# Regrouping the attention's products on TensorE: scores, values of two groups back, then transposes

## The chip, the cores and the metric

The kernel runs on one core of a Trainium2 chip. Its time is the device time of one execution in microseconds; of the kernel before there are three runs: 883.45, 883.65 and 884.38 us, median 883.65. Five engines work at once and meet by semaphores: TensorE (PE, products), VectorE (DVE), ScalarE (ACT), GpSimd (POOL) and SyncE (SP), whose queue issues most of the transfers.

## The reference

Windowed attention over 4 sequences of 576 positions with 8 heads of 64, then two dense networks on the 2304 positions:

```
scores = q @ k^T / 8, allowed where 0 <= query - key < 64
attn   = exp(scores - max) / (sum + 1e-9)
x      = attn @ v, heads side by side: 2304 x 512
x      = ((x @ w1) * (x @ w2)) @ w3 @ w_out          # w1, w2: 512 x 1024; w3: 1024 x 1024
h      = x @ w_in                                    # 512 x 2048
out    = (h * sigmoid(h)) @ w_out2                   # 2048 x 512
```

The weights are float64 arrays; their words are converted to float32 on the chip.

## The kernel before, in words

Attention is cut into 72 groups: 18 stretches of 128 positions times 4 pairs of heads, numbered so that the groups 12b to 12b+11 make up the 384 positions of block b (NBLK = 6 blocks). A group goes through these functions: `scores` (product of q and k into PSUM tile `s`, then on DVE, line 275, mask and row minimum into `sm`), `exps` (ACT, line 286), `normalise` (DVE: add, reciprocal and the multiply of line 298), `transposes` (three products with the identity, PSUM tile `t`, line 308), `split_t` (ACT and DVE bring the transposed weights to SBUF), `values` (product with v into PSUM tile `o`, and its sum into `xr`). Groups 0 to 16 are "plain" (float32 products, lines 261 and 335 to 337, a copy of `o` by ACT, line 338); the other 55 split each operand into a high and a low part (fp32r; lines 265, 269, 343, 344) and sum four parts of `o`: two ACT copies (347, 348), two DVE additions (349, 350), a POOL addition (351). `prep_qk` and `prep_v` make the high and low parts of q, k (ACT 240, POOL 244, DVE 247) and v (helper `split`, lines 79 and 82).

The program is in hand-written order: each engine executes its instructions in the order in which the code issues them. `half(2g)` and `half(2g+1)` issue the two halves of group g, and `halves_to` puts a half between other products. Three phases do so:

- `phase_w` (to about 104 us): DVE, ACT and POOL convert weight words (lines 114, 115, 125, 128, 132; the high and low parts at 140, 144), PE forms w3 x w_out (line 476, `accw`), and the first 28 halves run between. `fill` puts conversion steps between the steps of a softmax.
- `phase_a(b)`, one per block: 16 units of 12 products with w1, w2 (line 504, `ab`), then 8 units of 12 products with the formed weights (line 524, `x`). Before each of the 24 units one half of attention for the next block is issued, so a block carries twelve groups. Its input is `xr` split by `split_x` into `xa`, `xb`, a quarter at a time, in units 17, 19, 21 and 22 of the block before.
- after the last block, the second network (lines 627, 646).

PSUM holds one `s`, one `t` and one `o` tile; once the conversions of the first phase are done, odd groups use the tile `z` as a second `o`.

Of the kernel before, what the change touches and what calls it, by code (L numbers as in the profile page):

```python
# [42 lines left out]
def tile_window_attention_ffn(ctx, tc, qkv, vp, mask, ident, w1, w2, w3t, w_out, w_in, w_out2, out):  # L43
# [142 lines left out]


    NG = NU * NPAIR
    LAST_HALF = 2 * NG + 2
    qk_raw, v_raw, qk_st, v_st, s_st, p_st = {}, {}, {}, {}, {}, {}  # L190
    pt = {}

# [132 lines left out]
    def values(g):  # L325
        u, c = place(g)
        r = u % 3 * 128

        tag = "z" if done["step"] == len(line) and g % 2 else "o"
        o_ps = psa.tile([128, 2, 2, 128], F32, name=f"o{g}", tag=tag)  # L330
        if plain(g):


            v, p, o = v_p[g % 3], p_st.pop(g), o_ps[:, 0, 0]
            nc.tensor.matmul(o, lhsT=v[:, 0:128], rhs=p[:, 0:128], start=True, stop=False)
            nc.tensor.matmul(o, lhsT=v[:, 64:192], rhs=p[:, 128:256], start=False, stop=False)
            nc.tensor.matmul(o[:, 0:64], lhsT=v[:, 192:320], rhs=p[:, 256:320], start=False, stop=True)
            nc.scalar.copy(out=xr[:, c, r : r + 128], in_=o)
            return
        vhl = v_st.pop(g)  # L340
        b, a = pt[g % 2, 1], pt[g % 2, 0]
        for h in range(2):
            nc.tensor.matmul(o_ps[:, h], lhsT=vhl[:, h], rhs=b[:, h], start=(h == 0), stop=False)  # L343
        nc.tensor.matmul(o_ps[:, :, :, 0:64], lhsT=vhl[:, 2], rhs=a, start=False, stop=True)  # L344
        o_ps = o_ps.rearrange("p h t n -> p h (t n)")
        t = att.tile([128, 256], F32, name=f"ot{g}", tag="ot", bufs=1)
        nc.scalar.copy(out=t[0:64], in_=o_ps[64:128, 0, :])
        nc.scalar.copy(out=t[64:128], in_=o_ps[0:64, 1, :])
        nc.vector.tensor_tensor(out=t[0:64], in0=o_ps[0:64, 0, :], in1=t[0:64], op=ALU.add)
        nc.vector.tensor_tensor(out=t[64:128], in0=o_ps[64:128, 1, :], in1=t[64:128], op=ALU.add)  # L350
        nc.gpsimd.tensor_tensor(out=xr[:, c, r : r + 128], in0=t[:, 0:128], in1=t[:, 128:256], op=ALU.add)  # L351

    def half(h):


        g, odd = divmod(h, 2)
        if not odd:
            t_ps = transposes(g - 1) if 1 <= g <= NG else None
            if g < NG:
                scores(g)  # L360
            if t_ps is not None:
                split_t(g - 1, t_ps)
            if g < NG:
                exps(g)
        else:
            if g < NG:
                normalise(g)
            if 1 <= g <= NG:
                values(g - 1)
            for x in (g + 1, g + 2):  # L370
                if x - g == (1 if plain(x - 2) else 2):
                    prep_qk(x)
            if g < NG:
                prep_v(g)

            for x in range(g + 2, g + 5):
                if g < (x - 2 if plain(x - 2) else x - 4):
                    break
                load_qk(x)
            for x in range(g + 1, g + 4):  # L380
                if g < (x - 2 if plain(x - 3) else x - 3):
                    break
                load_v(x)

    halves = [0]

    def halves_to(n):
        while halves[0] < min(n, LAST_HALF):
# [3 lines left out]
    def split_x(blk, c):  # L392
        if c == 0:
            xhl[blk] = [slot(f"{t}{blk}", t, [2, 2, NB], F32R) for t in ("xa", "xb")]
        x = xhl[blk][c // 2][:, c % 2]
        split(x[:, 0], x[:, 1], xr[:, c], "dve", "dve" if blk else "pool")


    W_HALVES = 28
# [1 line left out]
    def phase_w():  # L401
# [58 lines left out]
        for s in range(16):  # L460
            sw, j = divmod(s, 8)
            loads_to(ready[s + 2] + (3 if s > 1 else 0))
            if j == 0:
                for i in range(4):
                    acc[i] = accumulator(f"accw{sw}_{i}", [128, 512])
            for part in range(2):
                first = ready[s + 1 if s else 0]
                steps_to(first + (ready[s + 2] - first) * (part + 1) // 2, (nc.vector, nc.gpsimd), 3)
                halves_to(min(W_HALVES, 2 + W_HALVES * (2 * s + part + 1) // 32))
                for c in range(4):  # L470
                    if halves[0] >= 6 * c + 8 and (0, c) not in split_done:
                        split_done.add((0, c))
                        split_x(0, c)
                fill(3)
                for i in (0, 1) if part == 0 else (2, 3):
                    nc.tensor.matmul(  # L476
                        acc[i], lhsT=w3x[s % 7][:, i * 128 : (i + 1) * 128], rhs=wo[:, j],
                        start=(j == 0), stop=(j == 7),
                    )
                    if j == 7:  # L480
                        n = sw * 4 + i
                        wp[n] = slot(f"wp{n}", f"w{16 + n}", [2, 512], F32R)
                        split(wp[n][:, 0], wp[n][:, 1], acc[i], "act", "dve")
# [272 lines left out]
```

## Time and profile before

| | |
|---|---|
| median of the runs | 883.65 us (883.45 to 884.38, 3 runs) |
| profiled execution | 884.13 us |
| its span, first to last instruction | 882.3 us |
| PE busy | 856.0 us, 97% |
| DVE, ACT, POOL busy | 480.7, 491.0, 430.6 us |
| mean granted TensorE clock | 0.997 of full speed |

The span is the time between the first and the last instruction of the profiled execution. A product's record begins when PE starts it and overlaps the next one's, so starts, not lengths, give its price. Stretches are in microseconds from the span's start. In a row of waits stands who waited, for whom, the total, how often, and the longest.

### The profile page before, as it was taken

Reading aid. Unit: us, or ns where it says so; the run is one execution under the profiler, and the core shown is the slowest. Engines: PE = TensorE matmul, PEld = TensorE weight load, DVE = VectorE, ACT = ScalarE, POOL = GpSimd, SP = SyncE. Lnnn points to the kernel's source line nnn. Section 1 sums busy time; section 2 is a strip of 40 time slices with the busy share of each in tenths; the row PEclk is TensorE's granted clock in tenths of the full one; section 3 lists DMA queues with packets and bytes.
Section 4 is the critical chain, followed back from the end, with each engine's and each line's share of the span. In section 5 each row is a group of like instructions: output and inputs, shape, how many; then the busy total and the mean of one; then the engine's idle time right before and its main releaser. Section 6 shows DMA issues by size and latency. Waiting matters only on the chain.

```text
span 882.3 us, 13255 instructions
## 1 busy us (share of the span) xinstructions
PE 856.0 (97%) x4362; PEld 737.0 (84%) x4362; DVE 480.7 (54%) x1202; ACT 491.0 (56%) x1219; POOL 430.6 (49%) x474
## 2 busy tenths in 40 slices
PE   4998999999999999999999999999999999999997
PEld 2454689999999999999999888888888888888896
DVE  5889888878888888888365886111111111111111
ACT  5778677788787788787475775222222222222322
POOL 4558476466466466465395787222322232222222
PEclk9999999999999999999999999999999999999999
DMA  8888423333432323331477500200020001000100
GB/s 286 295 251 262 134 79 99 125 99 100 127 94 90 126 90 100 119 99 50 182 277 261 202 0 1 77 20 0 1 89 7 0 1 51 22 0 1 48 1 25
DMA packets 43205, 85.84 MB, mean 97 GB/s; under 512 B 4864, under 2 KB 22528, under 8 KB 43136
## 3 DMA queue, kind: packets, MB, share of 16 engines
q1 hardware_dynamic: 37088, 75.55, 26.4%
q10 hardware_dynamic: 6048, 9.44, 2.9%
q8 instruction: 35, 0.57, 0.3%
q14 instruction: 34, 0.28, 0.1%
HBM read 75.53 MB, written 9.44 MB: 96 GB/s over the span
## 4 chain that ended last, share of the span: by engine, by line
PE 86%; DVE 2%; POOL 1%; issue 1%; ACT 0%; DMA 0%; POOLq 0%; SPq 0%; DVEq 0%
PE h L627 23%; PE o L646 22%; PE ab L504 21%; PE x L524 11%; PE t L308 2%; PE o L343 2%; PE s L265 1%; PE s L269 1%; PE accw L476 1%; PE o L344 1%; POOL klo L244 1%; DVE cv_b L128 0%; DVE cv_z L125 0%; DVE rs L294 0%; PE s L261 0%
## 5 line engine op out<-in xcount | busy, mean ns | idle before, releaser
L82 POOL TENSOR_TENSOR g<-sg,g 128x512 fp32r<-128x512 f32 (+1 forms) x80 | 94.8, 1185 | 250.0 <-ACT g L79 237.3
L627 PE MATMUL h<-x2t,hl 128*128 128x512 f32 (+1 forms) x960 | 213.4, 371 | 0.0
L646 PE MATMUL o<-hl,g 128*128 128x512 f32 x864 | 211.2, 392 | 0.4 <-ACT g L79 0.3
L633 DVE TENSOR_TENSOR sg<-h,sg 128x512 f32<-128x512 f32 (+1 forms) x80 | 51.1, 638 | 288.5 <-ACT sg L632 288.5
L627 PEld LDWEIGHTS h<-x2t,hl 128*128 128x128 f32 x960 | 169.4, 188 | 33.8
L646 PEld LDWEIGHTS o<-hl,g 128*128 128x128 f32 x864 | 160.9, 188 | 35.9 <-ACT g L79 0.8
L632 ACT ACTIVATE sg<-h 128x512 f32<-128x512 f32 (+1 forms) x80 | 44.4, 555 | 195.4 <-PE h L627 195.4
L504 PE MATMUL ab<-xa,hl 128*128 128x384 f32 x576 | 117.1, 338 | 0.0
L504 PE MATMUL ab<-xb,hl 128*128 128x384 f32 x576 | 115.6, 335 | 0.0
L504 PEld LDWEIGHTS ab<-xb,hl 128*128 128x128 f32 x576 | 101.4, 188 | 0.0
L504 PEld LDWEIGHTS ab<-xa,hl 128*128 128x128 f32 x576 | 99.8, 188 | 0.8
L351 POOL TENSOR_TENSOR xr<-ot 128x128 f32<-128x128 f32 x55 | 33.2, 603 | 118.5 <-DVE ot L350 116.5
L132 POOL TENSOR_TENSOR cv_b<-cv_b,cv_r 128x512 int32<-128x512 int32 x48 | 73.6, 1534 | 26.8 <-DVE cv_b L128 11.2
L79 ACT CAST g<-sg 128x512 fp32r<-128x512 f32 (+1 forms) x80 | 46.3, 579 | 63.5 <-DVE sg L633 61.8
L286 ACT ACTIVATE sm<-sm,nm 128x192 f32<-128x192 f32 x144 | 64.4, 448 | 17.7 <-DVE nm L275 16.6
L244 POOL TENSOR_TENSOR klo<-qk,qkhi 64x192 fp32r<-64x192 f32 x110 | 70.1, 637 | 5.7 <-ACT qkhi L240 1.5
L524 PE MATMUL x<-p,wp 128*128 128x384 f32 x360 | 69.6, 335 | 0.0
L524 PEld LDWEIGHTS x<-p,wp 128*128 128x128 f32 x360 | 62.2, 188 | 0.1
L125 DVE TENSOR_SCALAR cv_z<-cv_b 128x512 int32<-128x512 int32 x72 | 49.4, 686 | 17.0 <-ACT cv_b L114 16.6
L114 ACT ACTIVATE cv_b<-words 128x512 f32<-128x512 f32 x72 | 48.2, 670 | 11.5 <-DMA words<-in_w_out 5.6
L128 DVE SCALAR_TENSOR_TENSOR cv_b<-words,cv_z 128x512 int32<-128x512 int32 x72 | 49.4, 686 | 3.5 <-issue 0.5
L275 DVE CUSTOM_DVE_ANT_0 sm<-s,mask_sb 128x192 f32<-128x192 f32 x144 | 45.7, 354 | 6.6 <-PE s L261 3.6
(82 smaller groups left out, 1258.9 us busy)
## 6 DMA issues: line engine op xcount, KB each, us to landing
qk<-in_qkv SPq DMA_DIRECT2D x55, 384.0 KB, 3.1
words<-in_w_out SPq DMA_DIRECT2D x24, 512.0 KB, 8.4
words<-in_w3t SPq DMA_DIRECT2D x16, 512.0 KB, 6.2
words<-in_w SPq DMA_DIRECT2D x16, 512.0 KB, 6.2
words<-in_w_in SPq DMA_DIRECT2D x16, 512.0 KB, 6.8
v<-in_qkv SPq DMA_DIRECT2D x55, 96.0 KB, 2.7
x2d<-x2s ACTq DMA_DIRECT2D x24, 192.0 KB, 1.9
out_x<-osb ACTq DMA_DIRECT2D x18, 256.0 KB, 2.1
```

Source lines behind the costliest of these rows:

```text
L82: (nc.vector if eng_lo == "dve" else nc.gpsimd).tensor_tensor(out=lo, in0=src, in1=f32(hi), op=ALU.subtract)
L114: nc.scalar.activation(out=f32(self.b), in_=f32(self.high), func=AF.Copy, scale=2.0**-112)
L125: nc.vector.tensor_scalar(out=self.z, in0=b, scalar1=3, scalar2=None, op0=ALU.logical_shift_left)
L128: nc.vector.scalar_tensor_tensor(out=b, in0=self.high, scalar=-0x80000000, in1=self.z, op0=ALU.bitwise_and, op1=ALU.bitwise_or)
L132: nc.gpsimd.tensor_tensor(out=x, in0=b, in1=self.r, op=ALU.add)
L244: nc.gpsimd.tensor_tensor(out=k_lo[g % 2][hs, h * 192 : h * 192 + 192], in0=t[hs, n], in1=f32(hi[hs, n]), op=ALU.subtract)
L286: nc.scalar.activation(out=x, in_=x, func=AF.Exp, scale=-1.0, bias=nm[:, h : h + 1], accum_out=rs[:, h : h + 1])
L504: nc.tensor.matmul(acc, lhsT=w[:, l, fs], rhs=x[k // 2][:, k % 2, r, :], start=(k == 0 and n == 0), stop=(k == 3 and n == 2),)
L524: nc.tensor.matmul(acc, lhsT=wp[f][:, l, o * 128 : (o + 1) * 128], rhs=p[f][:, r, :], start=(f == 0 and n == 0), stop=(f == 7 and n == 2),)
L627: nc.tensor.matmul(acc, lhsT=weights["in", f // 4, k][:, l, fs], rhs=x[:, k, r, :], start=(k == 0 and i == 0), stop=(k == 3 and i == 2),)
L633: nc.vector.tensor_tensor(out=sg, in0=acc, in1=sg, op=ALU.mult)
L646: nc.tensor.matmul(oacc[t], lhsT=g[:, l, t * 128 : (t + 1) * 128], rhs=weights["out", f][:, r, :], start=(f == 0 and i == 0), stop=(f == 1 ...
```

## The change

On PE, the two clusters of a group (transposes of g-1 and scores of g in the even half, values of g-1 in the odd half) become one in the even half: scores of g, values of g-2, transposes of g-1. The sum of `o` is no longer issued by `values` itself: it is returned as a function and issued in the odd half behind `normalise`; at a block's last group it is issued at the end of the even half. There is one half more in all (`LAST_HALF`). The load of v is issued one group later for plain groups. `split_x` takes ACT for the high part and POOL for the low part in all blocks, and in the first phase it waits for two more halves.

```diff
--- before.py
+++ after.py
@@ -186,7 +186,7 @@
 
 
     NG = NU * NPAIR
-    LAST_HALF = 2 * NG + 2
+    LAST_HALF = 2 * NG + 3
     qk_raw, v_raw, qk_st, v_st, s_st, p_st = {}, {}, {}, {}, {}, {}
     pt = {}
 
@@ -335,38 +335,45 @@
             nc.tensor.matmul(o, lhsT=v[:, 0:128], rhs=p[:, 0:128], start=True, stop=False)
             nc.tensor.matmul(o, lhsT=v[:, 64:192], rhs=p[:, 128:256], start=False, stop=False)
             nc.tensor.matmul(o[:, 0:64], lhsT=v[:, 192:320], rhs=p[:, 256:320], start=False, stop=True)
-            nc.scalar.copy(out=xr[:, c, r : r + 128], in_=o)
-            return
+            return lambda: nc.scalar.copy(out=xr[:, c, r : r + 128], in_=o)
         vhl = v_st.pop(g)
         b, a = pt[g % 2, 1], pt[g % 2, 0]
         for h in range(2):
             nc.tensor.matmul(o_ps[:, h], lhsT=vhl[:, h], rhs=b[:, h], start=(h == 0), stop=False)
         nc.tensor.matmul(o_ps[:, :, :, 0:64], lhsT=vhl[:, 2], rhs=a, start=False, stop=True)
         o_ps = o_ps.rearrange("p h t n -> p h (t n)")
-        t = att.tile([128, 256], F32, name=f"ot{g}", tag="ot", bufs=1)
-        nc.scalar.copy(out=t[0:64], in_=o_ps[64:128, 0, :])
-        nc.scalar.copy(out=t[64:128], in_=o_ps[0:64, 1, :])
-        nc.vector.tensor_tensor(out=t[0:64], in0=o_ps[0:64, 0, :], in1=t[0:64], op=ALU.add)
-        nc.vector.tensor_tensor(out=t[64:128], in0=o_ps[64:128, 1, :], in1=t[64:128], op=ALU.add)
-        nc.gpsimd.tensor_tensor(out=xr[:, c, r : r + 128], in0=t[:, 0:128], in1=t[:, 128:256], op=ALU.add)
+
+        def total():
+            t = att.tile([128, 256], F32, name=f"ot{g}", tag="ot", bufs=1)
+            nc.scalar.copy(out=t[0:64], in_=o_ps[64:128, 0, :])
+            nc.scalar.copy(out=t[64:128], in_=o_ps[0:64, 1, :])
+            nc.vector.tensor_tensor(out=t[0:64], in0=o_ps[0:64, 0, :], in1=t[0:64], op=ALU.add)
+            nc.vector.tensor_tensor(out=t[64:128], in0=o_ps[64:128, 1, :], in1=t[64:128], op=ALU.add)
+            nc.gpsimd.tensor_tensor(out=xr[:, c, r : r + 128], in0=t[:, 0:128], in1=t[:, 128:256], op=ALU.add)
+
+        return total
 
     def half(h):
+
 
 
         g, odd = divmod(h, 2)
         if not odd:
-            t_ps = transposes(g - 1) if 1 <= g <= NG else None
             if g < NG:
                 scores(g)
-            if t_ps is not None:
-                split_t(g - 1, t_ps)
+            if 2 <= g <= NG + 1:
+                sums.append(values(g - 2))
+            if 1 <= g <= NG:
+                split_t(g - 1, transposes(g - 1))
             if g < NG:
                 exps(g)
+            if g >= 2 and (g - 2) % (3 * NPAIR) == 3 * NPAIR - 1:
+                sums.pop()()
         else:
             if g < NG:
                 normalise(g)
-            if 1 <= g <= NG:
-                values(g - 1)
+            if sums:
+                sums.pop()()
             for x in (g + 1, g + 2):
                 if x - g == (1 if plain(x - 2) else 2):
                     prep_qk(x)
@@ -378,11 +385,11 @@
                     break
                 load_qk(x)
             for x in range(g + 1, g + 4):
-                if g < (x - 2 if plain(x - 3) else x - 3):
+                if g < (x - 1 if plain(x - 3) else x - 3):
                     break
                 load_v(x)
 
-    halves = [0]
+    halves, sums = [0], []
 
     def halves_to(n):
         while halves[0] < min(n, LAST_HALF):
@@ -393,7 +400,7 @@
         if c == 0:
             xhl[blk] = [slot(f"{t}{blk}", t, [2, 2, NB], F32R) for t in ("xa", "xb")]
         x = xhl[blk][c // 2][:, c % 2]
-        split(x[:, 0], x[:, 1], xr[:, c], "dve", "dve" if blk else "pool")
+        split(x[:, 0], x[:, 1], xr[:, c], "act", "pool")
 
 
     W_HALVES = 28
@@ -468,7 +475,7 @@
                 steps_to(first + (ready[s + 2] - first) * (part + 1) // 2, (nc.vector, nc.gpsimd), 3)
                 halves_to(min(W_HALVES, 2 + W_HALVES * (2 * s + part + 1) // 32))
                 for c in range(4):
-                    if halves[0] >= 6 * c + 8 and (0, c) not in split_done:
+                    if halves[0] >= min(W_HALVES, 6 * c + 10) and (0, c) not in split_done:
                         split_done.add((0, c))
                         split_x(0, c)
                 fill(3)
```

In the order of PE, in block 1 (s, o, t: scores, values and transposes of the group whose number follows; ab: block products) before:

```order
L308 MATMUL t32_2422<-id_sb_70,sm0_72 128x128 x3
L265 MATMUL s33_2426<-qkhi33_2318 128x192 x2
L269 MATMUL s33_2426<-klo1_75,qkhi33_2318 128x384
L504 MATMUL ab1_14_2442<-xa1_1644,hl_855 128x384 x3
L504 MATMUL ab1_14_2442<-xa1_1644,hl_910 128x384 x3
L504 MATMUL ab1_14_2442<-xb1_1645,hl_1030 128x384 x3
L504 MATMUL ab1_14_2442<-xb1_1645,hl_1070 128x384 x3
L343 MATMUL o32_2460<-pt2_977,vhl32_2399 128x256 x2
L344 MATMUL o32_2460<-pt0_975,vhl32_2399 128x4x64
```

The values of group 32 stand twelve products behind its transposes. The same place on PE after the change:

```order
L265 MATMUL s33_2412<-qkhi33_2308 128x192 x2
L269 MATMUL s33_2412<-klo1_75,qkhi33_2308 128x384
L342 MATMUL o31_2420<-pt3_972,vhl31_2313 128x256 x2
L343 MATMUL o31_2420<-pt1_970,vhl31_2313 128x4x64
L308 MATMUL t32_2424<-id_sb_70,sm0_72 128x128 x3
L511 MATMUL ab1_14_2436<-xa1_1634,hl_849 128x384 x3
L511 MATMUL ab1_14_2436<-xa1_1634,hl_902 128x384 x3
```

Scores of 33 have moved ahead of the transposes of 32, and the values between them are those of group 31.

In the first phase on PE (accw: w3 x w_out) before:

```order
L308 MATMUL t3_370<-id_sb_70,sm1_73 128x128 x3
L261 MATMUL s4_374<-kp0_76,qk4_294 128x384
L476 MATMUL accw0_2_158<-wo_84,q_85 128x512
L476 MATMUL accw0_3_159<-wo_84,q_85 128x512
L476 MATMUL accw0_0_156<-wo_84,w3x0_88 128x512
L476 MATMUL accw0_1_157<-wo_84,w3x0_88 128x512
L335 MATMUL o3_414<-pw1_87,vp0_78 128x128
```

The transposes of group 3 stand first, the scores of group 4 behind them, and the values of group 3 four products later. The same place on PE after:

```order
L261 MATMUL s4_360<-kp0_76,qk4_288 128x384
L335 MATMUL o2_370<-pw0_86,vp2_80 128x128
L336 MATMUL o2_370<-pw0_86,vp2_80 128x128
L337 MATMUL o2_370<-pw0_86,vp2_80 128x64
L308 MATMUL t3_374<-id_sb_70,sm1_73 128x128 x3
L483 MATMUL accw0_2_158<-wo_84,q_85 128x512
L483 MATMUL accw0_3_159<-wo_84,q_85 128x512
```

Scores of 4 and values of 2 now stand ahead of the transposes of 3.

At a block's end on ACT after the change (ot: a part of the sum of `o`; xb: input of the next block; qkhi, vhl: preparation of later groups):

```order
L318 CAST pt2_971<-t36_2728 128x2x128
L320 CAST pt0_969<-t36_2728 64x64 x2
L286 ACTIVATE sm1_73,rs37_2721<-sm1_73,nm37_2720 128x192 x2
L348 COPY ot35_2740<-o35_2724 64x256
L349 COPY ot35_2740<-o35_2724 64x256
L79 CAST xb2_2547<-xr_83 128x384
L240 CAST qkhi39_2763<-qk39_2619 128x768
L79 CAST vhl37_2768<-v37_2544 128x3x64
```

The copies of the block's last group (35) stand behind the exponentials of 37, and the cast of the last quarter, which was DVE's (line 81), behind them.

## Rows read from the trace of the kernel before

**Rows 1.** busy us (instructions) of each engine by stretch, clock, DMA share, GB/s.
```profile
0.00:30.00 30.00, 17.70 (x46) 8.37 (x47) 17.25 (x41) 17.11 (x37) 14.81 (x21) 0.94 0.85 281
30.00:104.00 74.00, 66.20 (x231) 34.40 (x230) 66.77 (x145) 56.48 (x137) 50.78 (x41) 1.00 0.79 248
...
138.00:419.00 281.00, 280.86 (x1727) 275.14 (x1728) 232.08 (x749) 221.30 (x663) 160.31 (x242) 1.00 0.33 101
```

**Rows 2.** PE's waits from 0 to 123 us: total, times, longest.
```profile
PE t L308 <- DVE sm L298: 5.4, 6, 2.1
PE o L335 <- ACT pw L314: 2.8, 2, 1.9
PE t L308 <- ACT cv_b L114: 2.5, 1, 2.5
PE t L308 <- ACT cv_r L115: 2.3, 1, 2.3
```

**Rows 3.** PE in time, two block starts: start, us, engine, what.
```profile
237.81 0.49 PE L308 MATMUL t<-id_sb,sm 128*128 128x128 f32 x3
...
302.16 0.49 PE L308 MATMUL t<-id_sb,sm 128*128 128x128 f32 x3
...
302.89 1.20 PE L504 MATMUL ab<-xa,hl 128*128 128x384 f32 x6
303.93 1.20 PE L504 MATMUL ab<-xb,hl 128*128 128x384 f32 x6
```

**Rows 4.** PE in order of time, an unhindered values product and what follows.
```profile
310.46 0.40 PE L343 MATMUL o<-pt,vhl 128*128 128x256 f32 x2
...
310.81 0.50 PE L504 MATMUL ab<-xa,hl 128*128 128x384 f32 x2
```

**Rows 5.** line 81, 0 to 104 us: ns least/median/most, first to last start.
```profile
L81 DVE CAST xa<-xr x2: 1427/1434/1441, 36.4 to 54.0; 128x384 fp32r<-128x384 f32 x2
L81 DVE CAST xb<-xr x2: 1427/1434/1440, 74.5 to 95.1; 128x384 fp32r<-128x384 f32 x2
```

**Rows 6.** waits of SP's queue, 0 to 120 us.
```profile
SPq L229 <- PE o L337: 11.9, 11, 2.5
```

**Rows 7.** order of time on POOL and DVE near 74 us.
```profile
74.08 1.66 POOL L132 TENSOR_TENSOR cv_b<-cv_b,cv_r 128x512 int32<-128x512 int32 x1 [0.76 <-DVE rs L296]
...
75.89 0.68 DVE L125 TENSOR_SCALAR cv_z<-cv_b 128x512 int32<-128x512 int32 x1
```

**Rows 8.** line 81 on DVE, 138 to 425 us.
```profile
L81 DVE CAST xb<-xr x9: 359/361/506, 167.9 to 424.8; 128x384 fp32r<-128x384 f32 x9
```

**Rows 9.** line 82 on POOL, 138 to 425 us.
```profile
L82 POOL TENSOR_TENSOR p<-a,p x21: 1004/1015/1021, 137.7 to 395.8; 128x384 fp32r<-128x384 f32 x21
```

**Rows 10.** order of time at a block's end, all engines.
```profile
297.23 1.59 POOL L244 TENSOR_TENSOR klo<-qk,qkhi 64x192 fp32r<-64x192 f32 x2
...
297.79 0.37 ACT L318 CAST pt<-t 128x256 fp32r<-128x256 f32 x1 [0.40 <-PE s L269]
...
298.90 0.60 POOL L82 TENSOR_TENSOR vhl<-v,vhl 128x192 fp32r<-128x192 f32 x1
...
299.59 0.18 ACT L286 ACTIVATION_READ_ACCUMULATOR sm<-sm,nm 128x1 f32 x1
...
299.90 0.34 PE L344 MATMUL o<-pt,vhl 128*128 128x256 f32 x1
...
300.15 0.56 DVE L82 TENSOR_TENSOR xb<-xr,xb 128x384 fp32r<-128x384 f32 x1
...
301.10 0.84 ACT L240 CAST qkhi<-qk 128x768 fp32r<-128x768 f32 x1
...
301.84 0.35 ACT L79 CAST vhl<-v 128x192 fp32r<-128x192 f32 x1
...
302.36 0.48 ACT L529 COPY x2s<-x 128x384 f32<-128x384 f32 x1 [0.17 <-PE x L524]
...
302.55 0.58 POOL L351 TENSOR_TENSOR xr<-ot 128x128 f32<-128x128 f32 x1 [3.05 <-DVE ot L350]
```

## The prediction

> **What bounds the kernel now.** I first read the table of busy times by stretches [rows 1]. It shows two regimes. From 138 to 419 us (the blocks of the gated product, with attention for the next block between their products) PE is busy 280.86 of 281 us, and DVE, ACT and POOL have time left: only what PE itself executes can shorten it. From 30 to 104 us (weights converted, the product w3*w_out formed, attention of the first fourteen groups) PE is busy 66.20 of 74 us, DVE 66.77: neither is full, and they wait for each other. What runs from 427 us on holds no attention and is not touched.
>
> Second, the waits of PE over the first 123 us [rows 2]. Leaving aside the wait for the first transfer, nearly all stand ahead of the transposes of a group's softmax (5.4, 2.5 and 2.3 us) or of its values product (2.8 us); together 13.0. The reader is to see that a single one ahead of transposes lasts 2.5 us, though the scores of the next group, which need nothing from that softmax, are queued right behind it.
>
> Third, the order of time on PE within one block [rows 3, 4], which gives the price of an attention cluster.
>
> **The attention cluster where PE is full.** One block of the gated product runs from a transposes row at 237.81 to the first of the next block at 302.16, 64.35 us [rows 3]. It holds 288 block products; six take 303.93 - 302.89 = 1.04, so 0.173 each, 49.9 in all. It holds twelve groups; transposes and scores take 302.89 - 302.16 = 0.73, 8.8 in all. The rest, 64.35 - 49.9 - 8.8 = 5.7, is the twelve values products: 0.47 each. Where nothing holds them up they take 310.81 - 310.46 = 0.35 [rows 4]. The 0.12 between is PE catching up with operands that were finished just before: in the old order the values follow half a group behind the split of the transposes and of v. In the new order they read what was finished a group earlier, and they stand between scores and transposes, so one entry into attention per group takes the place of two. Each product of the new cluster should go at the pace it has in an unhindered place: 0.73 + 0.35 = 1.08 instead of 1.20. There are 55 groups of this kind: 55 x 0.12 = 6.6 us. Bounds: nothing, if the waits, now close together, cost the same bubbles; 0.47 x 55 cannot go, since the products stay; a little beyond 6.6 is possible where scores to values is a cheaper change than scores to block product. I take 6.6, because the unhindered row shows that the products need no more.
>
> The page "TensorE: Matmul & The Clock Gate" of the Trainium skill, section "The mechanism", says that weight loads overlap running products only when they use other row groups. By that each product would cost load plus stream wherever it stands, and this term would be 0. The trace disagrees: weight loads on all rows are busy 275.14 us of the same 281 in which the products are busy 280.86 [rows 1].
>
> **The first stage.** The transposes of group g-1 wait for its softmax's multiply on DVE. Before, scores of g stood behind that wait, so DVE's mask step, ACT's exponentials and the next multiply all started late. Now scores of g and values of g-2 are ahead of the wait: PE does them in it, and the softmax chain of g starts without it. The transposes come later by as much, which delays ACT's copy of them and the exponentials queued behind it where PE has no wait; the values have a group of slack against that.
>
> Second, DVE loses the four high-part casts of the block input: 2 + 2 of 1.43 us, 5.7 us [rows 5]. ACT gets four casts of about 0.5 (its copy of 128x384 takes 0.48 [rows 10]); it is busy 56.48 of 74 [rows 1] and hides them. Loads of v move one group later in the program, and SP no longer stands waiting for a values product half a group ahead: that wait is 11.9 us in eleven places [rows 6], with weight loads behind it. v is now read a group later, so the later load costs nothing.
>
> What can it give? PE idles 7.8 us between 30 and 104, and of the waits of [rows 2] the 2.3 ahead of transposes and a 1.9 ahead of values lie inside the first 30; 12.0 is the upper end. The other end is 0: PE waits as long for DVE's multiply, which stands behind the same conversions. DVE is 90% busy there, so its freed 5.7 us are the nearest row for the size. Not all of it reaches PE, as one cast falls where PE has work, but some of the early wait goes too. I take 6.0.
>
> The cast deserves a look. The one at 74.5 us took 1.43 while a POOL addition of 1.66, begun at 74.08, was running; the DVE operation behind it took 0.68 [rows 7]. In the later blocks such a cast takes 0.36 to 0.51 [rows 8]. "SBUF — State Buffer" of the Trainium skill, section "Who interferes with whom", has DVE and GpSimd lock a port pair for whole instructions. By that most of the 1.43 is waiting, which would pass to the next DVE operation that wants the pair: four times about 0.5, 2 us, would be freed, and the total would come out near 876. I keep the 5.7 as the size of what leaves DVE's queue, as the operation that follows shows no such wait.
>
> **The block's input.** In the later blocks the high part goes from DVE to ACT (20 casts of about 0.5) and the low part from DVE to POOL (1.015 us each by the like-sized subtraction [rows 9]). ACT is busy 221.30 and POOL 160.31 of 281 [rows 1], so both have room for the 10 and 20 us. What matters is the last quarter at each of five block ends. Its values now come with unit 22 instead of 21, its sum must pass, and the next block reads it at its tenth product. Available from the end of the values: 24 products of 0.173, a cluster of 1.08, nine products more, and the transposes behind the values, together about 7.0 us. Needed: from the values' end at 300.24 to the end of the sum at 303.13 it took 2.9 us before; ACT's split and exponentials of the same half now stand ahead (297.79 to 299.77, 2.0); then cast 0.5 and subtraction 1.0 [rows 9, 10]: 6.4 us. That leaves 0.6 us, where before the low part was ready at 300.71 for a use at 304.45. I put in 0.2 us for each of five ends, 1.0 in all, from bounds of 0 and the case below.
>
> **Sum.** The profiled execution took 884.13 us (span 882.3). 884.13 - 6.6 - 6.0 + 1.0 = 872.5. The median of the runs shown, 883.65, lies 0.5 below that execution, so 872.0.
>
> **Rivals.**
> - The first stage gives nothing (chance 0.17). DVE's queue is unchanged but for the casts, and DMA engines are busy 85% of the first 30 us [rows 1], so conversions may set the pace. Against: DVE idles 7.2 us from 30 to 104. Time: 872.0 + 6.0 = 878.0.
> - The cluster keeps its bubbles (0.14): the waits of five products stand together, and the six operands come from three engines; the rule on weight loads ends in the same place. Against: the unhindered row [rows 4]. Time: 872.0 + 6.6 = 878.6.
> - Both (0.10): the change doesn't do what it says, PE's waits only move from one product to another: 883.5 to 884.6.
> - Slower (0.09): the last quarter's chain is late at the block ends. If ACT runs the next preparation (0.84, 0.35) and a 0.48 copy first, and POOL its key subtractions (1.59) and the v subtraction (0.60) [rows 10], the chain grows by 3.9 us to 10.3; PE stands 3.3 us at each of five ends, 16.5 instead of 1.0: 872.0 + 15.5 = 887.5. It decides from about 2.5 us an end (the two gains, 12.6, over 5). For it: one in-order queue each, a margin of 0.6 us. Against: in the program's order the cast and the subtraction stand ahead of those preparations.
> - The forecast holds the remaining 0.50.
>
> **Range and chances.** The forecast's own range is 866 to 877: 12.0 instead of 6.0 at the low end, half of each gain at the high end. The two single rivals lie at 878 to 879. Leaving out most of the last two cases gives 865 to 882. A difference under about 0.2% (1.8 us) can't be told from none. Faster than that: 0.50 + 0.17 + 0.14 and a little of the case "both", 0.83; within: 0.08; slower: 0.09.
>
> **What would show it.** In the profile after: PE's waits ahead of transposes and values in the first 123 us down from 13.0 to about 6; the first block product at about 98 instead of 104; one attention cluster of about 1.08 us per group with a block period near 63.0 instead of 64.35; no POOL-released wait ahead of the values; at most a few tenths of idle PE before the tenth product of a block. I would be wrong on the first stage if the transposes' wait is as long as now; on the cluster if the values still take 0.47 or if the time reappears at the transposes; on the block ends if PE stands there for more than 1 us.

## The result and the profile after

The changed kernel takes 874.23 us (median of four runs, 872.4 to 877.79) where the kernel before took 883.73 beside it: ratio 0.9896, 95% interval 0.9864 to 0.9928. The profiled execution took 874.55 us (span 872.8) against the 884.13 from which the prediction's sum was made: 9.6 us less, where 11.6 was forecast (872.5).

Where the time went can be read from one row per block, the first block product in PE's order of time. The second of them in the profile after, with the values and the transposes ahead of it:

```profile
168.38 0.40 PE L342 MATMUL o<-pt,vhl 128*128 128x256 f32 x2
...
168.74 0.49 PE L308 MATMUL t<-id_sb,sm 128*128 128x128 f32 x3
168.99 1.31 PE L511 MATMUL ab<-xa,hl 128*128 128x384 f32 x6
```

The same row of every trace gives this table (start of the first block, then the length of each block, then from the start of the last stretch, which the change does not touch, to the last product; us):

| kernel | first block starts | block 0 | block 1 | block 2 | block 3 | block 4 | rest |
|---|---|---|---|---|---|---|---|
| before | 104.56 | 69.26 | 64.72 | 64.35 | 64.39 | 61.75 | 448.9 |
| after | 97.92 | 71.07 | 63.35 | 63.31 | 63.31 | 61.20 | 448.6 |
| v early | 99.09 | 67.93 | 63.31 | 63.29 | 63.31 | 61.20 | 448.6 |
| old casts | 100.77 | 72.55 | 67.44 | 67.35 | 65.88 | 62.61 | 448.6 |
| old casts, late | 101.27 | 70.12 | 64.33 | 64.33 | 64.34 | 61.55 | 448.6 |
| casts alone | 101.93 | 68.53 | 63.98 | 64.01 | 63.98 | 61.92 | 448.6 |
| two entries | 99.33 | 72.47 | 63.71 | 63.73 | 63.72 | 61.53 | 448.6 |
| copy early | 97.85 | 67.74 | 63.30 | 63.31 | 63.31 | 61.17 | 448.6 |
| sum first | 97.47 | 69.94 | 70.30 | 70.30 | 70.34 | 68.37 | 448.6 |
| prep first | 99.27 | 67.51 | 63.31 | 63.35 | 63.36 | 61.20 | 448.6 |

So the change gives 6.6 us in the first stage, takes back 1.8 in block 0, and gives 4.0 in blocks 1 to 4 (1.4, 1.0, 1.1, 0.5). Of the 0.7 left, 0.3 is in the table's last column and 0.4 behind the last product.

How far such a figure repeats can be read here too. Up to the first block product, after, v early and prep first execute the same instructions in the same order, yet it starts at 97.92, 99.09 and 99.27; in old casts and old casts, late it is 100.77 and 101.27. With one trace of each kernel, a difference of the first stage below about 1.4 us shows nothing. Blocks 1 to 4 repeat to 0.05 us.

**By stretches**, as in [rows 1]: busy us (instructions) of PE, PEld, DVE, ACT, POOL, then granted clock, DMA share, GB/s.

```profile
30.00:98.00 68.00, 63.44 (x226) 33.95 (x224) 60.52 (x138) 55.72 (x136) 49.15 (x40) 1.00 0.79 252
138.00:412.00 274.00, 274.00 (x1715) 273.25 (x1714) 213.43 (x709) 223.88 (x676) 172.74 (x261) 1.00 0.33 102
```

PE was idle 7.8 us of its 74 between 30 us and the first block; now it is idle 4.6 of 68. In the blocks it is never idle, and weight loads fill 273.25 of the 274 us. DVE fell from 0.83 to 0.78 of the time there, ACT and POOL rose a little.

**PE's waits up to 117 us**, as in [rows 2]: total, times, longest.

```profile
PE o L335 <- ACT xr L338: 2.6, 3, 1.6
PE t L308 <- DVE sm L298: 2.3, 2, 1.6
PE s L265 <- DVE qkhi L247: 1.7, 1, 1.7
...
PE t L308 <- ACT cv_r L115: 1.2, 1, 1.2
```

Ahead of transposes and values: 2.6 + 2.3 + 1.2 = 6.1, against 13.0 before. The wait for qkhi (the low part of q, from DVE) is a new one; it falls in block 0. It comes with the early place of the scores: where the transposes stand first (before, casts alone, two entries) it is 0.2 us, and PE waits longer ahead of the transposes instead (1.0 to 2.5 us in block 0, against 0.7 here). The new order shows on DVE in the first row of a softmax, the mask step. In both traces up to 98 us it reads (busy us, mean ns, then DVE's idle time ahead of it); before:

```profile
L275 DVE CUSTOM_DVE_ANT_0 sm<-s,mask_sb 128x192 f32<-128x192 f32 x27 | 8.6, 353 | 3.3 <-PE s L261 3.2
```

and after:

```profile
L275 DVE CUSTOM_DVE_ANT_0 sm<-s,mask_sb 128x192 f32<-128x192 f32 x29 | 9.2, 352 | 0.2 <-PE s L261 0.2
```

DVE no longer stands waiting for scores that PE held back behind the previous softmax: 3.3 us became 0.2, and two more mask steps are done by then. Whether the first stage owes its gain to that is asked under "Two entries" below.

**At a block's end**, as in [rows 10], the last quarter of the block's input on all engines (idle time before it, and what ended it, in brackets):

```profile
290.03 0.29 PE L343 MATMUL o<-pt,vhl 128*128 128x256 f32 x1
...
294.06 0.46 POOL L352 TENSOR_TENSOR xr<-ot 128x128 f32<-128x128 f32 x1 [0.34 <-DVE ot L351]
...
294.56 0.51 ACT L79 CAST xb<-xr 128x384 fp32r<-128x384 f32 x1 [1.53 <-POOL xr L352]
...
295.15 1.01 POOL L82 TENSOR_TENSOR xb<-xr,xb 128x384 fp32r<-128x384 f32 x1 [0.62 <-ACT xb L79]
```

From the end of the values (290.32) to the low part (296.16) it takes 5.8 us. PE in the same stretch:

```profile
295.40 0.49 PE L308 MATMUL t<-id_sb,sm 128*128 128x128 f32 x3
295.65 1.31 PE L511 MATMUL ab<-xa,hl 128*128 128x384 f32 x6
296.80 1.20 PE L511 MATMUL ab<-xb,hl 128*128 128x384 f32 x6
```

The six products from 295.65 and the first four from 296.80 are the first ten of the block; by the order of the three passes the tenth reads the last quarter's high part, and the eleventh is the first to read the low part. It starts four products behind 296.80, at about 297.5: a margin of 1.3 us, and PE waits there at no block end. Scores and values also cover DVE's multiply here. It ends at 294.98, when PE is already at the scores, and the transposes that need it come at 295.40:

```profile
294.42 0.56 DVE L298 TENSOR_TENSOR sm<-sm,rs 128x384 f32<-128x384 f32 x1
...
294.64 0.36 PE L265 MATMUL s<-qkhi 128*128 128x192 f32 x2
...
295.04 0.40 PE L342 MATMUL o<-pt,vhl 128*128 128x256 f32 x2
```

**In block 0** two things are new. SP's queue, ACT and PE:

```profile
108.82 15.68 SPq L217 DMA_DIRECT2D qk<-in_qkv  x3
124.55 0.42 SPq L233 DMA_DIRECT2D v<-in_qkv  x1
```

```profile
127.57 0.35 ACT L79 CAST vhl<-v 128x192 fp32r<-128x192 f32 x1 [4.34 <-DMA v<-in_qkv]
```

```profile
115.63 0.44 PE L265 MATMUL s<-qkhi 128*128 128x192 f32 x2 [1.72 <-DVE qkhi L247]
```

The first v that has to be split is now loaded behind three loads of q and k which stand waiting, most of the time for DVE's subtraction (line 247) and for PE's scores, which still read what they overwrite; ACT stands 4.3 us for it, with the copy of the transposes and the exponentials queued behind. And behind the 1.72 us of waiting for the low part of q, PE runs for some microseconds at the lower of its two clock levels (1.2 instead of 2.4 GHz); from 116 to 120 us the granted share is 0.58 and 0.56 (by stretches, as above):

```profile
116.00:118.00 2.00, 2.00 (x12) 2.00 (x11) 1.45 (x6) 0.51 (x1) 1.98 (x2) 0.58 0.49 134
118.00:120.00 2.00, 2.00 (x9) 2.00 (x8) 0.34 (x2) 1.74 (x6) 0.70 (x1) 0.56 0.16 63
```

### The profile page after: what moved, and what is told of

Its sections match the earlier page's. It is cut to its first block, busy times and chain, and to the rows that moved or that the text cites. A ratio compares the mean times of both kernels' runs of the same rounds, so it can differ in the third digit from the quotient of the medians.

```text
span 872.8 us, 13349 instructions
## 1 busy us (share of the span) xinstructions
PE 849.9 (97%) x4362; PEld 738.5 (85%) x4362; DVE 454.2 (52%) x1158; ACT 498.4 (57%) x1243; POOL 445.3 (51%) x494
## 4 chain that ended last, share of the span: by engine, by line
PE 84%; POOL 1%; issue 1%; DVE 1%; DMA 0%; ACT 0%; POOLq 0%; SPq 0%
PE h L634 23%; PE o L653 22%; PE ab L511 21%; PE x L531 12%; PE t L308 2%; PE o L342 1%; PE s L265 1%; PE s L269 1%; PE o L343 1%; POOL klo L244 0%; DMA v<-in_qkv 0%; POOL p L82 0%; POOL cv_b L132 0%; DVE rs L294 0%; POOL hl L144 0%
## 5 line engine op out<-in xcount | busy, mean ns | idle before, releaser
L511 PE MATMUL ab<-xa,hl 128*128 128x384 f32 x576 | 120.1, 343 | 0.0
L244 POOL TENSOR_TENSOR klo<-qk,qkhi 64x192 fp32r<-64x192 f32 x110 | 67.2, 611 | 8.6 <-ACT qkhi L240 4.4
L115 ACT ACTIVATE cv_r<-words 128x512 int32<-128x512 uint32 x72 | 47.8, 664 | 0.0
```

Source lines behind the costliest of these rows:

```text
L244: nc.gpsimd.tensor_tensor(out=k_lo[g % 2][hs, h * 192 : h * 192 + 192], in0=t[hs, n], in1=f32(hi[hs, n]), op=ALU.subtract)
L511: nc.tensor.matmul(acc, lhsT=w[:, l, fs], rhs=x[k // 2][:, k % 2, r, :], start=(k == 0 and n == 0), stop=(k == 3 and n == 2),)
```

## The experiments

Edits are to the changed kernel unless said. My theory throughout was the prediction's: the saving in the blocks comes from values whose operands are a group old, the saving in the first stage from scores that no longer stand behind a softmax and from DVE's casts.

**v early: is block 0's loss the late load of v?**

```
-                if g < (x - 1 if plain(x - 3) else x - 3):
+                if g < (x - 1 if plain(x) else x - 3):
                     break
                 load_v(x)
```

> The changed kernel, but v of the split groups (17 and later) is loaded as early as before. Theory: in the changed kernel the load of v for group 17 stands in SP's queue behind two q/k loads that wait for DVE, lands at 127.5 us, and ACT waits 4.3 us for it; that is where the block from 98 to 168 us lost 1.5 us against the kernel before. Then ACT's wait for v is gone here, that block takes about 68 us instead of 70.1, and the time is about 872, 2 below the changed kernel's 874.2. Rival: that block is late because DVE makes the low part of q for group 17 late (PE waits 1.7 us for it); then the time stays at 874.

872.9 us (870.99 to 873.42), ratio to before 0.9872 (0.9852 to 0.9892). Block 0 falls from 71.07 to 67.93, and ACT waits for no v. (The first block product comes 1.2 us later than in the changed kernel; nothing ahead of it was changed.) But the load accounts for only half of that. From the values at 124.48 to the scores two groups on at 136.36 the changed kernel needs 11.88 us, this one (124.03 to 134.42) 10.39: 1.5 us. The other 1.6 us is the clock in the profiled execution. The wait for the low part of q is still here and as long, yet the clock stays at 2.4 GHz behind it:

```profile
116.77 0.44 PE L265 MATMUL s<-qkhi 128*128 128x192 f32 x2 [1.71 <-DVE qkhi L247]
...
119.42 1.20 PE L511 MATMUL ab<-xb,hl 128*128 128x384 f32 x6
```

```profile
118.00:120.00 2.00, 2.00 (x16) 2.00 (x15) 1.08 (x4) 1.45 (x6) 1.85 (x2) 1.00 0.63 197
```

From those scores to the second run of six products takes 119.42 - 116.77 = 2.65 us; in the changed kernel 119.86 - 115.63 = 4.23. The same wait (1.71 to 1.73 us) stands in old casts, old casts late, copy early and sum first, and the granted clock is 1.00 behind it in all four: one trace of six shows the fall. It is not shown to belong to the change. So 1.5 us is shown for the late load, and the intervals of the two kernels' ratios overlap.

**Old casts: what do the engines of the block input's split give?**

```
-        split(x[:, 0], x[:, 1], xr[:, c], "act", "pool")
+        split(x[:, 0], x[:, 1], xr[:, c], "dve", "dve" if blk else "pool")
```

> The changed kernel with the block input split as before (high part on DVE, low part on DVE in later blocks). Theory: the four casts of 1.43 us on DVE are most of what the first stage gained; then the first block product moves from 98 to about 102 us and the time is about 878. Rival: the order of the products on PE gave the first stage its gain, and the casts were covered; first block product at 98 to 99, time 874 to 875.

892.41 us (891.27 to 895.33), ratio 1.0104 (1.0081 to 1.0126): slower than before, which neither theory nor rival had. The first stage ends at 100.77, so with the casts left on DVE 3.8 of its 6.6 us remain (3.3 by the first stage of the next experiment, which is the same); its mask step waits no more for scores, as in the changed kernel:

```profile
L275 DVE CUSTOM_DVE_ANT_0 sm<-s,mask_sb 128x192 f32<-128x192 f32 x28 | 8.8, 352 | 0.4 <-PE s L261 0.4
```

The loss is at the block ends, in order of time:

```profile
304.33 0.46 POOL L352 TENSOR_TENSOR xr<-ot 128x128 f32<-128x128 f32 x1 [1.96 <-DVE ot L351]
...
304.82 0.74 DVE L81 CAST xb<-xr 128x384 fp32r<-128x384 f32 x1 [0.57 <-POOL xr L352]
...
305.60 0.83 DVE L82 TENSOR_TENSOR xb<-xr,xb 128x384 fp32r<-128x384 f32 x1
...
307.13 0.56 DVE L298 TENSOR_TENSOR sm<-sm,rs 128x384 f32<-128x384 f32 x1
...
307.83 0.52 PE L308 MATMUL t<-id_sb,sm 128*128 128x128 f32 x3 [2.41 <-DVE sm L298]
```

The last quarter's split on DVE waits for POOL's sum and stands ahead of the multiply of the next softmax, whose transposes PE has next. PE's waits for that multiply are 10.3 us in four places from 138 to 430 us. Behind some of them the clock falls too: between 240 and 244 us the granted share is 0.70, and six products then take 1.92 us instead of 1.04 (242.12 to 244.04, the start of the next six):

```profile
240.49 0.52 PE L308 MATMUL t<-id_sb,sm 128*128 128x128 f32 x3 [2.51 <-DVE sm L298]
...
242.12 2.12 PE L511 MATMUL ab<-xb,hl 128*128 128x384 f32 x6
```

**Old casts, late: is it that wait in DVE's queue?** The same kernel, the last quarter's split one attention unit later:

```
-if blk + 1 < NBLK and o == 3 and f == 0:
+if blk + 1 < NBLK and o == 3 and f == 4:
```

> The kernel with the old split on DVE (892.4), with the split of the block's last quarter issued one unit later, behind the odd half with its softmax multiply. Theory: DVE waits in its queue for the sum of the last group, and the softmax's multiply stands behind that wait, so PE waits 2.4 us for it at each block end and then runs some twenty products at half clock; with the multiply ahead of the wait the block takes 63.3 to 64 us instead of 67.4, and the time is 877 to 880. Rival: the quarter itself comes too late on DVE (cast 0.7 and subtraction 0.8 after the sum); then it is later still here, PE waits at a block's tenth product, and the time stays at 890 or more.

882.29 us (880.36 to 886.85), ratio 0.9995 (0.9982 to 1.0008). The time that theory gave, 877 to 880, and its 63.3 to 64 us for a block are missed, but the mechanism shows: the blocks go from 67.4 to 64.33, and at the same place PE waits 0.50 us instead of 2.41:

```profile
299.07 0.56 DVE L298 TENSOR_TENSOR sm<-sm,rs 128x384 f32<-128x384 f32 x1
299.77 0.52 PE L308 MATMUL t<-id_sb,sm 128*128 128x128 f32 x3 [0.50 <-DVE sm L298]
300.39 0.65 DVE L81 CAST xb<-xr 128x384 fp32r<-128x384 f32 x1
```

The multiply (299.07) now stands ahead of the cast. A block is still 1.0 us longer than with the casts on ACT. By PE's starts 0.66 of that lies ahead of these transposes, and 0.34 is spread over block products; there the rival's wait shows too, 0.25 us ahead of the weights of the eleventh product, for DVE's subtraction.

**Casts alone: the kernel before, with the split on ACT and POOL.**

```
-        split(x[:, 0], x[:, 1], xr[:, c], "dve", "dve" if blk else "pool")
+        split(x[:, 0], x[:, 1], xr[:, c], "act", "pool")
```

> The kernel before with the new split of the block input alone (ACT and POOL). Theory (casts count): first block product at about 100 instead of 104.6, time 879 to 880. Rival (order counts): at 104, time 883. The later blocks stay at 64.35 us each under both.

879.6 us (877.45 to 881.18), ratio 0.9957 (0.9938 to 0.9976). The time is as theory had it, the first block product is not: 101.93 where about 100 was said. The first stage ends 2.6 us earlier, not 5.7. DVE did lose 5.7 us of casts (its busy time up to the first block product falls from 84.6 to 78.4 us), but waits longer for scores in return, 5.7 us instead of 3.3 up to 98 us:

```profile
L275 DVE CUSTOM_DVE_ANT_0 sm<-s,mask_sb 128x192 f32<-128x192 f32 x28 | 8.9, 355 | 5.7 <-PE s L261 5.6
```

Blocks 0 to 3, which I had expected unchanged, are 0.3 to 0.7 us shorter each, block 4 is 0.2 longer. In block 2 the difference is in the values: their twelve clusters, each read to the next block product, take 4.82 us instead of 5.24. Between 175 and 360 us the weight loads of the values wait for the low part of v (POOL) for 0.8 us in two places, where before it was 2.5 us in twelve.

**Two entries: is it the age of the operands or the single cluster?** Values two groups back, but in the odd half, with block products between them and the scores, as before:

```
+            t_ps = transposes(g - 1) if 1 <= g <= NG else None
             if g < NG:
                 scores(g)
-            if 2 <= g <= NG + 1:
-                sums.append(values(g - 2))
-            if 1 <= g <= NG:
-                split_t(g - 1, transposes(g - 1))
+            if t_ps is not None:
+                split_t(g - 1, t_ps)
...
         else:
+            if 2 <= g <= NG + 1 and (g - 2) % (3 * NPAIR) != 3 * NPAIR - 1:
+                sums.append(values(g - 2))
```

> The changed kernel with two clusters per group as before (transposes and scores in the even half, values in the odd half), but values of two groups back. Theory: what the cluster saved in the later blocks is the wait for operands just made, not the number of entries; then a block takes 63.3 us as in the changed kernel, a values product 0.35. Rival: one entry instead of two saves it; then 64.35 as in the kernel before, a values product 0.47. For the first stage: scores again stand behind the transposes' wait, so if that order gave the gain the first block product is back at 101 to 104, and the time 877 to 880; if not, 98 and 874.

879.16 us (878.56 to 879.7), ratio 0.9948 (0.9934 to 0.9963). PE in order of time, a group in a block's middle:

```profile
271.71 0.49 PE L308 MATMUL t<-id_sb,sm 128*128 128x128 f32 x3
...
274.52 0.40 PE L342 MATMUL o<-pt,vhl 128*128 128x256 f32 x2
274.76 0.28 PE L343 MATMUL o<-pt,vhl 128*128 128x256 f32 x1
274.88 1.24 PE L513 MATMUL ab<-xa,hl 128*128 128x384 f32 x6
```

Values take 0.36 here with two entries into attention. In the trace before, the same stretch has them at

```profile
272.66 0.40 PE L343 MATMUL o<-pt,vhl 128*128 128x256 f32 x2
272.89 0.34 PE L344 MATMUL o<-pt,vhl 128*128 128x256 f32 x1
273.07 1.23 PE L504 MATMUL ab<-xa,hl 128*128 128x384 f32 x6
```

0.41: the third product starts 0.23 behind the first in either, but takes 0.18 instead of 0.12. Over a whole block the same holds: from the first of the three products to the next product of another kind it takes 0.44 on average before (5.24 us in block 2), 0.35 here and 0.36 in the changed kernel; in old casts, late, with the single cluster and the casts still on DVE, it is 0.36 too. So older operands, not one entry instead of two, make the values cheap. A block is still 0.4 us longer than in the changed kernel (63.72 against 63.31), and that is a pause at its end, where the transposes stand ahead of the scores: nine products begun at 296.55 take 1.56, to 298.11, and then

```profile
298.49 0.52 PE L308 MATMUL t<-id_sb,sm 128*128 128x128 f32 x3 [0.21 <-ACT xb L79]
```

0.38 later. Without it the block would take 63.3 us, as with the single cluster, whose transposes come behind scores and values. So the place of the transposes at a block's end is the cluster's own share.

The expectation also asked about the first stage, and there the answer goes against my theory. The scores stand behind the transposes' wait again, and DVE's mask step waits for them as before:

```profile
L275 DVE CUSTOM_DVE_ANT_0 sm<-s,mask_sb 128x192 f32<-128x192 f32 x28 | 8.9, 354 | 3.5 <-PE s L261 3.3
```

Yet the first block product comes at 99.33, not back at 101 to 104. That is where v early and prep first have it (99.09, 99.27), with the scores ahead, and 1.4 us behind the changed kernel, no more than traces of one and the same first stage differ. So a gain from the early place of the scores is not shown. What is larger than that spread is the step from casts alone (101.93) to this kernel: 2.6 us with values of two groups back and what goes with them (the sum issued later, the load of v and the split of the block's input in the first phase too). PE's wait ahead of the values for ACT's copy of the transposes, 2.8 us before and 1.3 with casts alone, is gone here.

**Copy early: is the new wait of the values for ACT's copy worth anything?** With v early, the copy of a plain group's output goes ahead of the exponentials.

```
                 split_t(g - 1, transposes(g - 1))
+            if sums and plain(g - 2):
+                sums.pop()()
             if g < NG:
                 exps(g)
```

> The kernel with v loaded early (872.9), in which ACT copies the values of the plain groups in the even half, ahead of the exponentials, instead of behind the odd half's multiply. Theory: PE's three waits in the first stage for that copy (2.7 us in all), which the changed kernel has in place of others, come from one PSUM tile freed late; they go, the first block product comes 1 to 2 us earlier, time 871 to 872. Rival: the first stage is held by DVE and the transfers; the waits move to the transposes, the time stays at 873.

872.59 us (871.5 to 873.3), ratio 0.9883 (0.9867 to 0.99), as v early. The wait for xr (2.7 us there) is gone; in its place stands

```profile
PE t L308 <- DVE sm L298: 5.4, 4, 1.9
```

where v early has 0.9 (total us, times, longest). The first block product, at 97.85, is 1.2 us ahead of v early's, as theory said, but not ahead of the changed kernel's 97.92, whose first stage is v early's: a gain is not shown. The rival fits better: the wait moves, as the exponentials now stand behind the copy.

**Sum first: do the output sums have to stand behind the multiply?** With v early, every sum at the end of the even half:

```
-            if g >= 2 and (g - 2) % (3 * NPAIR) == 3 * NPAIR - 1:
+            if sums:
                 sums.pop()()
```

> The kernel with v loaded early (872.9), but all output sums issued at the end of the even half, ahead of the softmax's multiply, as the changed kernel does at a block's last group only. Theory: DVE's two additions wait for ACT's copies behind the exponentials, so the multiply comes about 0.9 us later, but it has 1 to 2 us to spare; blocks stay at 63.3 us and the time at 873. Rival: placing the sums behind the multiply is what keeps PE from waiting for the transposes; then blocks take 64 us or more and the time is 877 or more.

903.9 us (901.55 to 905.67), ratio 1.0233 (1.0213 to 1.0254): each block 7 us longer. My theory, that the place of the sums makes no difference, fell. In order of time:

```profile
271.75 0.42 DVE L350 TENSOR_TENSOR ot<-o,ot 64x256 f32<-64x256 f32 x1 [0.94 <-ACT ot L349]
...
273.04 0.56 DVE L298 TENSOR_TENSOR sm<-sm,rs 128x384 f32<-128x384 f32 x1
...
273.74 0.52 PE L308 MATMUL t<-id_sb,sm 128*128 128x128 f32 x3 [0.64 <-DVE sm L298]
```

DVE's additions wait for ACT's copies, which stand behind two exponentials; the multiply waits behind the additions, and PE waits for it in nearly every group (22.8 us in 38 places from 138 to 430).

**Prep first: what remains in block 0.** With v early, the preparation of q and k ahead of the multiply at two groups:

```
+            first = [x for x in (g + 1,) if g in (PLAIN - 1, PLAIN)]
+            for x in first:
+                prep_qk(x)
             if g < NG:
                 normalise(g)
```

> The kernel with v loaded early, with one more step moved: at groups 16 and 17 the preparation of the next group's q and k (ACT's cast, the subtractions of DVE and POOL) stands ahead of the softmax's multiply in the odd half instead of behind it and the sums. Theory: what is left of block 0's excess is PE's single wait for the low part of q (1.7 us ahead of scores at about 115 us, 0.7 more for k's) and the stretch at half clock behind it, and that wait comes from DVE's multiply (1.40) standing ahead of the 0.70 subtraction. Then the wait goes below 0.5 us, the products behind it stay at 0.17 each, block 0 goes from 67.9 to 65 to 66.5 us, the time to 870 to 871.5. Rival: the load of q and k itself is late (it is two transfers in 7.5 us, issued just before), or DVE's multiply now stands behind a subtraction that waits for it, so PE's wait only moves to the transposes: block 0 stays at 67 to 69, time 872 to 874.

872.58 us (871.62 to 872.79), ratio 0.9872 (0.9856 to 0.9889): block 0 67.51, the time as with v early. The rival held. The wait is halved, not gone:

```profile
PE s L269 <- POOL klo L244: 1.2, 2, 0.6
PE s L265 <- DVE qkhi L247: 0.9, 1, 0.9
```

because DVE's subtraction now itself stands waiting for ACT's cast:

```profile
114.45 1.52 DVE L247 TENSOR_TENSOR qkhi<-qk,qkhi 64x256 fp32r<-64x256 f32 x1 [0.89 <-ACT qkhi L240]
```

## Why the prediction was right, and where its parts were not

Direction and size held: 872.0 was forecast, 874.23 measured. The mechanism held in the blocks; in the first stage the size came out near and the stated cause did not. The parts, in its order:

- **The attention cluster (-6.6): the step held, its size was about a quarter too large.** By the prediction's way of counting, the whole cluster came to (63.31 - 49.9) / 12 = 1.12 us, where 1.08 was said and 1.20 taken for before: 0.09 saved instead of 0.12, 55 x 0.09 = 4.8 us. The term that was mis-sized is the values before the change, 0.47. It was a remainder, and it had taken in some 0.3 us per block of the block products, which average 0.1744 and not 0.173. Read from their starts the values took 0.44 (5.24 us in twelve), and after the change they go at the unhindered pace (168.38 to 168.74, 0.36, as [rows 4]). A change from transposes to other products has a price too, but it is an old one: six block products behind transposes take 296.80 - 295.65 = 1.15 us against 1.04 behind scores [rows 3], and before it was the scores that paid it, 302.89 - 302.40 = 0.49 behind transposes against 295.04 - 294.64 = 0.40 now. The row of before:

```profile
302.40 0.45 PE L265 MATMUL s<-qkhi 128*128 128x192 f32 x2
```

  The reason given, operands that were finished just before, is borne out by the two entries, and "one entry in place of two" is not what pays.
- **Weight loads.** The Trainium skill, "TensorE: Matmul & The Clock Gate", section "The mechanism", has a sentence that lets loads overlap products only from other row groups; a sentence above it in the same section also lets a load into the background weight buffer go ahead. Loads on all rows are busy 273.25 of 274 us in which PE is never idle, so the first sentence alone does not describe this kernel, after as before. Which buffer the loads go to, no run shows.
- **The first stage (-6.0): -6.6 here, and -5.5 and -5.3 in the two other traces of the same first stage; that the sum came so near is in part luck.** The waits ahead of transposes and values fell to 6.1 (about 6 was said), and the first block product came at 97.92 (98). But two steps failed. "DVE's freed 5.7 us are the nearest row for the size": the casts give 2.6 alone. "Now scores of g and values of g-2 are ahead of the wait", so the chain of softmaxes starts earlier: with the scores back behind the wait (two entries) the stage still ends at 99.33, so what the scores give does not stand out from the 1.4 us by which one and the same first stage differs. Values of two groups back with what goes with them, beside the casts, are what the runs show (101.93 to 99.33); the prediction had no number for them. No run has the scores first with values of one group back, so how the rest divides stays open.
- **The cast's 1.43.** The Trainium skill, "SBUF — State Buffer", section "Who interferes with whom", made about 2 us of it real, and the 2.6 lies nearer to that than to my 5.7. The trace agrees in that number only: the casts left DVE whole (84.6 to 78.4 us busy), no operation behind them grew by them, and what they left became waiting for scores (3.3 to 5.7 us). Why such a cast takes 1.43 us there and 0.36 in the later blocks, no run shows.
- **Block ends (+1.0): nothing.** Chain 5.8 us against the 6.4 estimated, margin 1.3 instead of 0.6; 0.2 of that is that the low part is first read by the eleventh product, not the tenth. The sum no longer stands behind the preparation of q and k. The price of the slow rival is real all the same: with the split left on DVE each end costs 2.4 to 2.9 us of PE's time and the kernel is slower than before. It comes by another way than the rival said, by the multiply queued behind the split.
- **"The later load costs nothing": false.** In block 0 it costs 1.5 us, as it is issued behind loads that wait. The half clock behind the wait for the low part of q costs another 1.6 in the profiled execution, and nothing in my steps spoke of it; it is not shown to belong to the change.
- **By place**, measured against forecast, with 0.12 per group and 0.2 per block end: the first stage 0.6 us better, block 0 2.7 worse, blocks 1 to 4 0.7 worse, and outside 0.7 better. That is the 2.0 us between 872.5 and 874.55.
- **The range.** Half of each gain at the high end is 872.0 + 3.3 + 3.0 = 878.3, not the 877 that was stated; the measured time lies below either.

So the sum by what was measured: -6.6 in the first stage, +1.8 in block 0, -4.0 in the other blocks, -0.7 outside: 9.6 less than 884.13 gives the 874.55 of the profile.

The versions with v early have the lowest medians (872.9, with copy early or prep first 872.6), but their intervals overlap that of the changed kernel: that they beat it is not shown.

## What to carry to other kernels

Where PE is full, give a product operands that were finished a whole step earlier, and put what needs none of them ahead of the product that waits. Ask of each wait which engine's queue it holds up in turn. A step that is moved takes its DMA's place in an in-order queue with it: look at what stands ahead of it there. And when an operation leaves an engine, its own duration does not tell the gain: four casts of 5.7 us gave 2.6 in the first stage, as the engine then waited longer for something else, while at a block's end a split of 1.6 us, left on DVE, cost up to 4.1 us a block, the fall of the clock included, as it stood waiting ahead of what PE needed. And take two traces of the same work before a difference of a microsecond is given a cause.

## What the runs showed of the hardware

- The same wait of PE (1.71 to 1.73 us ahead of the same scores) was followed by a granted clock of 0.58 and 0.56 in two stretches of 2 us in one trace and of 1.00 in five others. At block ends of the old casts a wait of 2.51 us had 0.70 behind it, one of 2.41 had 1.00. What decides between the levels these runs do not show; the cost, some 1.6 us, comes on top of the wait.
- Three transposes cost whatever follows them about 0.1 us: six block products take 1.15 us behind them and 1.04 behind scores, the three scores products 0.49 behind them and 0.40 behind block products.
- The same instructions up to the first block product took 97.92, 99.09 and 99.27 us in three traces.
